# A fused recurrence and gated MLP: the first pairs' sums freed of a shared-tile dependency, all steps in another order, and an earlier gate for the third pair's inputs

## The chip, the cores and the metric

The kernel runs on one core of one Trainium2 chip. The metric is the device time of one execution in microseconds (us), the median of several runs. Five engines work side by side, each with its own queue in program order: TensorE (PE, with the weight loads PEld shown apart), VectorE (DVE), ScalarE (ACT), GpSimd (POOL) and SyncE (SP). Here SP issues nearly all transfers of inputs and outputs, POOL issues the weight transfers, and sixteen DMA engines move the data.

## What is computed

Two parts follow each other. The first is a recurrence with a 48x48 state per batch and head, whose decay differs by row. The second is an MLP on its output, with the gate h cos(h).

```python
batch, n_heads, seq, head_dim = (4, 8, 768, 48)
for t in range(S):
    state = alpha[:, :, t, :, None] * state + np.einsum('bhd,bhe->bhde', k[:, :, t], v[:, :, t])
    y[:, :, t] = np.einsum('bhd,bhde->bhe', q[:, :, t], state)
x = attn_out.transpose(0, 2, 1, 3).reshape(B * S, H * D)   # 3072 x 384
h = x @ w_in            # w_in 384 x 2048
g = h * np.cos(h)
return (g @ w_out)      # w_out 2048 x 384
```

## The kernel before

**Pairs.** The 4 x 768 tokens are cut into 12 *pairs* J of 256 tokens; three pairs make one batch (`NJB = 3`), and the state passes from pair to pair within a batch. Each of the 128 partitions holds two neighbouring tokens, e = 0 and 1. A pair is worked as two chunks c = 0 and 1 of 128 tokens.

**The steps of one pair**, each a small function that issues a handful of instructions:

- `load a|k|q|v` (SP, one DMA of 384 KB each). `ln` (ACT) takes the logarithm of alpha.
- `cums` (PE) sums these logs over the tokens with a triangular matrix. For pairs 0, 1 and 2 the two tokens have their own sums: `cums0` makes those of e = 0 and `cums` those of e = 1, in the two banks of one PSUM tile `cums_h` (`two_banks`). For pairs 3 to 11 `mula` (POOL) multiplies the two tokens' alphas first, `cums` makes one set of sums in the tile `x`, and `sub` (DVE) derives the other.
- `icp J e` and `exps J e` (ACT) read a bank of sums and write exp of minus and plus the sums. For pairs 3 to 11 `eb` is all four of them and then `ln` of the next pair.
- `sk J e`, `sq J e` scale k and q by these (kh, qh), on POOL or DVE. `castv` (POOL) casts v; `vst` (four DMAs from SP) or, for pairs 0 to 2, `vpe` (PE) with `vev` (ACT) stacks it in another order. `decay` (POOL) prepares the factors of the state.
- `trans` (PE, 32 transposes), `evT J c` (DVE or ACT, the copy of a bank to qkT), `scores J c` (PE), `mask J c` (DVE), `outer` (PE, the pair's additions to the state, U), `add` (DVE) and `state` (POOL) carry the state on.
- `yT` (PE) makes the output of the recurrence, transposed; `evy J c` copies it to xT.
- The MLP: `m1 J u` for u = 0 to 3 (PE, 12 matmuls of 256 columns, 512 hidden features), `sin` (ACT, the cosine), `gate` (DVE, the product), then `m2 J c part` (PE, 4 matmuls of 384 columns), `evo J c` (copy) and `out J c` (store).

In the profile a step is seen by its line and its tile: `cums` L160 and L172, `icp` L197, `exps` L205, `trans` L272, `scores` L287, `outer` L305, `yT` L354, `m1` L374, `sin` L380, `gate` L385, `m2` L403. The weights come in eight blocks, `w1 u` (L126) and `w2 u` (L132), called W1.u and W2.u below; m1 of block u needs W1.u, and part u of m2 needs W2.u.

**PSUM.** The tag `h` has three buffers of two banks, shared by `cums_h`, U, the stacked v, the transposes T, the scores A, y and the hidden tile h. A new tile waits until all readers of the buffer's previous tile are done. The tags `x` and `o` have one buffer each; so m2 of the next chunk waits for the copy of the last one.

**Order.** Nothing is scheduled by the framework: the table `PLAN` (L446 to L511) gives every step of every pair a number, the steps are issued in the order of these numbers, and a letter behind a number names the engine (`12160:D` is DVE). Each engine works through its own share of the list strictly in that order. `IDLE` places matmuls on a tile of zeros between the first steps. Dependencies between steps are found from the tiles that they touch, and a PSUM tile counts as a whole there: an instruction of ACT that reads one bank of `cums_h` comes after every matmul to the other bank that stands before it in the list, and a matmul after every such read.

**The gate.** `GATES` makes the load of alpha of pair 2 (`a`, 2) wait for the last matmul of a step; the loads behind it in SP's queue wait with it:

```python
GATES, AFTER = {("a", 2): ("yT", 1)}, {}
...
if (nm, J) in AFTER:
    tc.add_manual_dep(dma.ins, AFTER[nm, J].ins.name, ...)
```

Of the kernel before, what the change touches and what calls it, by code (L numbers as in the profile page):

```python
# [11 lines left out]
AF = mybir.ActivationFunctionType  # L12
# [4 lines left out]
def kernel(  # L17
# [10 lines left out]
    nc = tc.nc  # L28
    B, H, S, D = q.shape
# [69 lines left out]
    GATES, AFTER = {("a", 2): ("yT", 1)}, {}  # L99
# [57 lines left out]
    def sums(J, t, mats):  # L157
        o = t[:, 0:HD].rearrange("p (h d) -> p h d", h=H)
        for i, m in enumerate(mats):
            nc.tensor.matmul(o, m.rearrange("p c i -> p (c i)"), lna_t[J % NL][:, i, :, 0:D], start=(i == 0),  # L160
                             stop=(i == len(mats) - 1))

    def cums(J):
        if (J, 1) not in cums_ps:
            cums_ps[J, 1] = ps.tile([C, 512], FP, tag="x", name="cums", bufs=1)
        t = cums_ps[J, 1]
        lna = lna_t[J % NL]
        ne = 1 if J in both else 2
        sums(J, t, [tri, tri][:ne])
        for p in range(NP):  # L170
            for e in range(ne):
                nc.tensor.matmul(t[:, HD + 2 * p : HD + 2 * p + 2],  # L172
                                 lna[:, e, 2 * p : 2 * p + 2, :].rearrange("s h d -> s (h d)"), inchunk,
                                 start=(e == 0), stop=(e == ne - 1))
# [4 lines left out]
    def cums0(J):  # L179
        t = two_banks("cums_h")  # L180
        for e in range(2):
            cums_ps[J, e] = t[:, e]
        sums(J, cums_ps[J, 0], [tri, strict])
# [10 lines left out]
    def icp(J, e):  # L194
        act_set("exp")
        icp_sb[J, e] = sb.tile([C, HD], FP, tag=f"icp{e}", name="icp", bufs=BUF["cp"])
        nc.scalar.activation(out=icp_sb[J, e], in_=logs(J, e)[:, 0:HD], func=AF.Exp, scale=-1.0)  # L197

    def exps(J, e):
# [5 lines left out]
        nc.scalar.activation(out=cp_sb[J, e], in_=t[:, 0:w], func=AF.Exp)  # L205
# [219 lines left out]
    def idle(n):  # L425
# [21 lines left out]
        "load a": "1320 1974 27415 27985 34270 40270 43270 54870 67336 68770 70970 93397",  # L447
        "load k": "750 2544 28555 37270 46270 52480 58570 69470 72470 85140 91627 113474",
        "load q": "5250 6750 29125 38770 48970 56370 57870 60070 78470 84570 87104 96187",
        "load v": "3750 8250 35770 41770 51910 61570 67906 73970 75470 85710 95267 96757",  # L450
        "w1": "15334 12769 17804 16954",
        "w2": "11919 20284 19434 21134",
        "mula": "- - - 36680 41180 47582 54280 61956 76220 87867 79850 105765",
        "ln": "6160 7660 35857 38802 - - - - - - - -",
        "cums0": "7065 8565 36762 - - - - - - - - -",
        "cums": "7385 8885 37082 40224 45645 52564 65189 75864 86319 101370 105687 126624",
        "sub": "- - - 41095 48653 53084 68143 79971 86910 101948 106207 127144",
        "icp 0": "8400 10365 37282 - - - - - - - - -",
        "icp 1": "9990 9615 38042 - - - - - - - - -",
        "exps 0": "11510 9085 37657 - - - - - - - - -",  # L460
        "exps 1": "10740 11125 38417 - - - - - - - - -",
        "eb": "- - - 43138 49360 59320 71283 83790 88947 103219 109067 127741",
        "sk 0": "8970:D 11125:D 38180 44230 53330 64626 74150 90547 93387 106715 109595 129364:D",
        "sk 1": "10655:D 10185:D 38612:D 45094:D 52380 60226 77170 88817 96837 110545 113395 132041",
        "sq 0": "12160:D 14753:D 40150:D 45680:D 56671:D 65155:D 78900 85074 95107 111495 112445 133161",
        "sq 1": "12974:D 14283:D 39680:D 45680 55230 63676 75100 86024 91497 114515 116415 129403",
        "castv": "10660 16184 42680 48680 62906 71716 73380 94337 92617 104995 130491 144063",
        "vst": "- - - 49610 63836 82270 79970 98527 102027 109974 131421 151922",
        "vpe": "12269 19888 44159 - - - - - - - - -",
        "vev": "15703:A 20408:A 45777:A - - - - - - - - -",  # L470
        "decay": "11579 11749 45180 49450 56180 80800 76050 92447 114345 115465 132991 146818",
        "trans": "14073 17773 40885 47348 58944 70064 80866 92234 109989 116249 127239 136001",
        "evT 0": "14773:A 18473:A 41585 48048 60976 71899 81566:A 93894 111044 116949:A 129834 138061",
        "evT 1": "16453:A 19403:A 43330 48048:A 59896 72979 81586 93289 112124 117657 128759 137201:A",
        "scores 0": "16168 19573 43514 48885 69514 73578 83495 102418 118225 127719 141861 153101",
        "scores 1": "17553 21293 45302 49948 60920 83715 87697 106082 118445 127019 136481 141641",
        "mask 0": "16608 20013 43954 49603 70759 74158 85295 104038 118665 130439 144246 155872",
        "mask 1": "17993 21808 46625 51218 62056 84155 88867 106682 120280 127619 136921 143106",
        "outer": "11844 21513 43734 50168 69734 87367 83935 102638 115919 118665 142081 152771",
        "add 0": "13808 22948 46150 50743 70284 87917 86435 103563 117182 119805 142631 155397",  # L480
        "add 1": "15551 24515 - 53559 72504 - 88392 107822 - 121420 145386 -",
        "state 0": "14460 23600 46802 51395 70936 89767 87087 104215 121237 120457 143283 156049",
        "state 1": "18654 43450 - 61176 78120 - 96057 115635 - 131261 146038 -",
        "yT": "20503 26545 48000 58219 72693 91349 90719 109104 124433 140168 151138 162701",
        "evy 0": "21333:D 27535:D 49128:D 60501:D 73683 92814:D 91919 110094:D 125423 140998 152879:D 163777:D",
        "evy 1": "21333 27658 48990 59421:D 73683:D 92339:D 91549 110569:D 125793 141368 152128 163814",
        "m1 0": "23356 30719 52864 63871 77482 95445 98081 113200 130658 146436 158652 170128",
        "m1 1": "22038 32037 51246 65489 74546 94127 92809 121714 129340 147754 154722 171446",
        "m1 2": "27430 29401 54182 61235 78800 96763 104369 120396 132629 149072 159970 166198",
        "m1 3": "25132 33355 55500 62553 76164 99399 110564 111882 136796 145118 161288 172764",  # L490
        "sin 0": "24874 32237 54382 65389 79000 96963 99659 114718 132212 147954 160232 171646",
        "sin 1": "23556 33555 52906 67007 76064 95645 94327 123232 131204 149332 156240 172964",
        "sin 2": "28948 30919 55700 62866 80318 98281 106765 121914 134147 150590 161488 167716",
        "sin 3": "26650 40836 57018 64071 77682 100917 112613 113621 138314 146636 162806 174282",
        "gate 0": "26130 33386 55531 67003 80446 98112 100808 116042 133493 149103 161381 172795",
        "gate 1": "24990 37307 54055 68618 77213 96794 95476 124381 132353 150481 157389 174113",
        "gate 2": "30097 32068 57141 64015 82191 99430 108297 125521 135296 151739 162637 168865",
        "gate 3": "28010 42190 58281 65863 78831 102423 113762 114902 139463 147785 164252 175431",
        "m2 0 0": "28748 41460 56818 70639 84360 100717 114518 125318 138114 150390 163586 174082",
        "m2 0 1": "34673 42113 57471 71292 85013 101670 115171 125971 138767 152023 164239 176046",  # L500
        "m2 0 2": "35326 42766 59519 71945 85666 103063 116824 128034 139420 153416 164892 176699",
        "m2 0 3": "35979 44554 60172 73893 86619 103716 117477 128687 140893 154069 165545 177352",
        "m2 1 0": "37612 45947 66807 80118 88012 106397 119090 131976 142506 156040 167516 174735",
        "m2 1 1": "38265 46600 67460 81441 88665 107050 119743 133947 143159 156693 168169 175393",
        "m2 1 2": "38918 49200 68113 82094 89318 107703 123032 134600 143812 157346 168822 178005",
        "m2 1 3": "39571 50593 68766 82747 89971 108356 123685 135253 144465 157999 169475 178658",
        "evo 0": "36832:D 45407 61581:D 78353:D 87472 105178:D 118330 129540 141746 154922:D 166398:D 178205:D",
        "evo 1": "40620:D 52358:D 69619 83600:D 99289 111649:D 124538 136831 148962 159862 170328:D 179531:D",
# [49 lines left out]
```

## Time and profile before

| what | value |
|---|---|
| median of 3 runs | 186.13 us (185.88 to 186.54) |
| the profiled execution | 185.82 us, its span 184.0 us |
| PE busy | 175.6 us, of it 66.8 in m1 (L374) and 66.7 in m2 (L403) by the page |
| DVE, ACT, POOL busy | 134.7, 126.4, 77.3 us |
| ACT table loads | 18 of 1.28 us |
| one load of 384 KB, issue to landing | about 6 us (median) |
| W1 and W2 blocks, issue to landing | 7.1 and 10.2 us (median) |
| first m1 matmul | 21.72 us |
| last PE work ends | 180.9 us |

The page divides the span into 40 slices of 4.6 us; a digit is the busy share in tenths. Busy time of PE is modelled, since matmuls overlap, so a stall is better seen in the distance between the starts of steps. A bracket behind a row of the timeline gives the idle time ahead of it on its engine, and who ended it.

### The profile page before, as it was taken

How to read it: one execution, taken by the hardware profiler on the slowest of the kernel's cores; microseconds unless marked ns; L12 is line 12 of the kernel's file. 1: busy time of each engine (PE TensorE's matmuls, PEld its weight loads, DVE VectorE, ACT ScalarE, POOL GpSimd, SP SyncE). 2: the span in 40 equal slices, each digit the busy share in tenths (PEclk: the TensorE clock that was granted, in tenths of full speed). 3: DMA queues.
4: the chain of work that ended last, by engine and by line, in shares of the span. 5: the costliest groups of instructions: out<-in, count | busy, mean ns of one | idle time of the engine just before them, and what ended most of it. 6: DMA issues, size and time to landing. Idle time of an engine off the chain costs nothing.

```text
span 184.0 us, 5751 instructions
## 1 busy us (share of the span) xinstructions
PE 175.6 (95%) x2469; PEld 125.7 (68%) x2469; DVE 134.7 (73%) x184; ACT 126.4 (69%) x161; POOL 77.3 (42%) x110
## 2 busy tenths in 40 slices
PE   7888899998999999999999999999999999999993
PEld 2435678664687776876688668586876686786872
DVE  7078876589999889599659986975976656763561
ACT  2466976889698986889678999728965273372330
POOL 5079610147763743792994168830550320100000
PEclk9999999999999999999999999999999999999999
DMA  5999999999959999997799943500050004302102
GB/s 148 261 260 164 185 201 226 258 248 264 298 135 278 264 221 233 264 264 198 174 277 266 266 124 86 145 0 4 4 181 8 2 9 138 133 0 75 56 0 86
DMA packets 60137, 29.47 MB, mean 160 GB/s; under 512 B 51024, under 2 KB 60112, under 8 KB 60112
## 3 DMA queue, kind: packets, MB, share of 16 engines
q1 hardware_dynamic: 56256, 25.86, 58.1%
q0 software_dynamic: 3712, 3.15, 11.2%
q8 instruction: 19, 0.31, 0.8%
q10 hardware_dynamic: 144, 0.10, 0.2%
q14 instruction: 6, 0.05, 0.1%
HBM read 25.17 MB, written 4.72 MB: 162 GB/s over the span
## 4 chain that ended last, share of the span: by engine, by line
PE 73%; ACT 16%; DVE 3%; DMA 3%; issue 2%; SPq 1%; POOL 0%
PE h_ps L374 30%; PE o_ps L403 26%; PE y_ps L354 5%; DMA a<-in_alpha_dram 3%; ACT c_sb L380 3%; PE T_ps L272 3%; PE A_ps L287 3%; ACT L141 3%; ACT lna L146 3%; ACT cp L205 2%; ACT L380 2%; ACT qkT L278 2%; PE U_ps L305 2%; ACT icp L197 2%; PE o_last L403 1%
## 5 line engine op out<-in xcount | busy, mean ns | idle before, releaser
L385 DVE TENSOR_TENSOR gsb<-h_ps,c_sb 128x1024 bf16<-128x1024 f32 x48 | 58.0, 1220 | 21.8 <-ACT c_sb L380 21.2
L380 ACT ACTIVATE c_sb<-h_ps,halfpi 128x1024 bf16<-128x1024 f32 x48 | 53.0, 1113 | 27.6 <-PE h_ps L374 24.0
L374 PE MATMUL h_ps<-xT,w 128*128 128x256 bf16 x576 | 66.8, 273 | 0.4 <-DVE us L319 0.3
L403 PE MATMUL o_ps<-w,gsb 128*128 128x384 bf16 x368 | 66.7, 327 | 0.0
L374 PEld LDWEIGHTS <-w 128*128 128x128 bf16 x576 | 55.4, 98 | 9.4 <-issue 0.8
L403 PEld LDWEIGHTS <-gsb 128*128 128x128 bf16 x400 | 36.4, 98 | 21.4 <-DVE gsb L385 0.4
L327 POOL TENSOR_TENSOR un<-us,c 128x384 bf16<-128x384 f32 x20 | 16.7, 836 | 38.4 <-DVE us L319 27.5
L293 DVE TENSOR_TENSOR A_sb<-A_ps,msk 128x1024 bf16<-128x1024 f32 x24 | 28.9, 1213 | 2.0 <-PE A_ps L287 2.0
L217 POOL TENSOR_TENSOR kh<-k,icp 128x384 bf16<-128x384 f32 x17 | 16.9, 1000 | 8.5 <-ACT icp L197 8.5
L221 POOL TENSOR_TENSOR qh<-q,cp 128x384 bf16<-128x384 f32 x15 | 15.3, 1026 | 11.0 <-ACT cp L205 11.0
L154 POOL TENSOR_TENSOR a<-a 128x384 f32<-128x384 f32 x9 | 9.0, 1000 | 13.3 <-DMA a<-in_alpha_dram 13.3
L224 POOL CAST vp<-v 128x768 bf16<-128x768 f32 x12 | 10.1, 839 | 9.3 <-DMA v<-in_v_dram 7.9
L146 ACT ACTIVATE lna<-a 128x768 bf16<-128x768 f32 x12 | 10.2, 846 | 4.7 <-DMA a<-in_alpha_dram 4.7
L429 PE MATMUL idle_ps<-zeros 128*128 128x512 bf16 x40 | 11.5, 429 | 1.2 <-DVE halfpi L77 1.2
L141 ACT ACT_TABLE_LOAD x9 | 11.5, 1283 | 0.9 <-PEq L542 0.7
L278 ACT COPY qkT<-T_ps 128x1024 bf16<-128x1024 bf16 x8 | 8.0, 1015 | 5.9 <-PE T_ps L272 5.8
L380 ACT ACT_TABLE_LOAD x9 | 11.5, 1283 | 0.2
L319 DVE TENSOR_TENSOR us<-U_ps,un 128x384 f32<-128x384 f32 x16 | 8.7, 548 | 3.9 <-PE U_ps L305 2.9
L415 DVE COPY o_sb<-o_ps 128x384 f32<-128x384 f32 x12 | 6.6, 552 | 6.7 <-PE o_ps L403 6.7
L278 DVE COPY qkT<-T_ps 128x1024 bf16<-128x1024 bf16 x16 | 10.7, 675 | 0.0
L287 PE MATMUL A_ps<-qkT 48*128 48x128 bf16 x192 | 9.2, 218 | 1.0 <-ACT vs L244 0.6
L287 PEld LDWEIGHTS <-qkT 48*128 48x128 bf16 x192 | 5.8, 94 | 5.5 <-issue 3.1
(68 smaller groups left out, 153.7 us busy)
## 6 DMA issues: line engine op xcount, KB each, us to landing
k<-in_k_dram SPq DMA_DIRECT2D x12, 384.0 KB, 6.0
a<-in_alpha_dram SPq DMA_DIRECT2D x12, 384.0 KB, 5.7
v<-in_v_dram SPq DMA_DIRECT2D x12, 384.0 KB, 6.2
q<-in_q_dram SPq DMA_DIRECT2D x12, 384.0 KB, 6.3
out_dram<-o_sb SPq DMA_DIRECT2D x23, 192.0 KB, 3.7
vs<-vp SPq DMA_DIRECT2D x36, 64.0 KB, 2.4
w<-in_moe_w_out_dram POOLq DMA_DIRECT2D x4, 384.0 KB, 10.2
w<-in_moe_w_in_dram POOLq DMA_DIRECT2D x4, 384.0 KB, 7.1
```

What stands on the lines that cost most here:

```text
L141: nc.scalar.preload_act_table_set("natural_log_exp_and_others")
L146: nc.scalar.activation(out=lna_t[J % NL][:, :, :, 0:D].rearrange("p e h d -> p h e d"), in_=a_sb.pop(J), func=AF.Ln)
L217: eng.tensor_tensor(out=kh_t[J % NQ][:, e, :, 0:D], in0=kqv["k", J][:, :, e], in1=icp_, op=ALU.mult)
L221: eng.tensor_tensor(out=qh_t[J % NQ][:, e, :, 0:D], in0=kqv["q", J][:, :, e], in1=cp, op=ALU.mult)
L278: ins = copy(out=qkT_sb[J][:, c], in_=T_ps[J][:, c].rearrange("r n e s -> r n (e s)"))
L287: last = nc.tensor.matmul(A_ps[J, c][:, a, p, :], qkT[r, c, NP + p, :], qkT[r, c, p, :], start=True, stop=True)
L293: nc.vector.tensor_tensor(out=A_sb[J][:, c].rearrange("s a p t -> s (a p) t"), in0=A_ps.pop((J, c)).rearrange("s a p t -> s (a p) t"), in1 ...
L327: nc.gpsimd.tensor_tensor(out=u, in0=U_sum.pop(n), in1=c2_sb[J][:, :, c].unsqueeze(3).to_broadcast([C, NP, 2, D]), op=ALU.mult)
L374: nc.tensor.matmul(h_ps[J, u][:, f, :], w1[:, kk, ft * C : (ft + 1) * C], xT[J][:, kk, :], start=(kk == 0), stop=(kk == KT - 1))
L380: nc.scalar.activation(out=c_sb[J, u], in_=h_ps[J, u], func=AF.Sin, bias=halfpi, scale=1.0)
L385: nc.vector.tensor_tensor(out=gsb[J][:, u * FW : (u + 1) * FW], in0=h_ps.pop((J, u)), in1=c_sb.pop((J, u)), op=ALU.mult)
L403: nc.tensor.matmul(o[:, 0 : cols.stop - cols.start], gsb[J][:, ft, c * C : (c + 1) * C], w2[:, ft, cols], start=(done == 1 and ft == fts[0 ...
```

## The change

Three things are changed. First, for pairs 0 to 2 the matmuls and the reads of the two banks of `cums_h` are recorded by token (`use`), and an ACT read of one token's bank and a PE write of the other's are declared free of each other. Second, the gate of pair 2's alpha is the step `yT` of pair 0 in place of pair 1. Third, `PLAN` and `IDLE` are new throughout: every step has another number, and some have another engine.

```diff
-    GATES, AFTER = {("a", 2): ("yT", 1)}, {}
+    GATES, AFTER = {("a", 2): ("yT", 0)}, {}
...
+    users = {}
+
+    def use(J, e, ins, pe=False):
+        for e2, pe2, other in users.setdefault(J, []):
+            if e2 != e and pe2 != pe:
+                tc.declare_no_dep(ins.ins, other.ins, reason="the two tokens' sums lie in banks of their own")
+        users[J].append((e, pe, ins))
+
-    def sums(J, t, mats):
+    def sums(J, t, mats, e=1):
...
+            if (J, 0) in cums_ps:
+                use(J, e, ins, pe=True)
...
-        sums(J, cums_ps[J, 0], [tri, strict])
+        sums(J, cums_ps[J, 0], [tri, strict], e=0)
...
-        nc.scalar.activation(out=icp_sb[J, e], in_=logs(J, e)[:, 0:HD], func=AF.Exp, scale=-1.0)
+        ins = nc.scalar.activation(out=icp_sb[J, e], in_=logs(J, e)[:, 0:HD], func=AF.Exp, scale=-1.0)
+        if (J, 0) in cums_ps:
+            use(J, e, ins)
```

The matmuls of `cums` and the ACT instruction of `exps` are recorded in the same way. Of the plan, the rows that the steps below speak of (one number per pair, 0 to 11; the old row above the new one):

```diff
-        "load a": "1320 1974 27415 27985 34270 40270 43270 54870 67336 68770 70970 93397",
+        "load a": "10 30 960 1010 1230 1770 2160 1940 2610 3070 3560 3090",
-        "load k": "750 2544 28555 37270 46270 52480 58570 69470 72470 85140 91627 113474",
+        "load k": "40 150 1140 1490 1990 2230 2050 3290 2740 4070 3580 4640",
-        "w1": "15334 12769 17804 16954",
+        "w1": "400 380 500 160 - - - - - - - -",
-        "w2": "11919 20284 19434 21134",
+        "w2": "650 1000 490 970 - - - - - - - -",
-        "sk 1": "10655:D 10185:D 38612:D 45094:D 52380 60226 77170 88817 96837 110545 113395 132041",
+        "sk 1": "250:D 320:D 1220 1580 2100 2320 2890 3300 3660 4300 4470 5300",
-        "sq 0": "12160:D 14753:D 40150:D 45680:D 56671:D 65155:D 78900 85074 95107 111495 112445 133161",
+        "sq 0": "330:D 470 1130:D 1610 2110 2520 2860 3460 3640 4290 4340 5150",
-        "trans": "14073 17773 40885 47348 58944 70064 80866 92234 109989 116249 127239 136001",
+        "trans": "350 510 1330 1630 2120 2550 3040 3480 4370 4630 5060 5320",
-        "outer": "11844 21513 43734 50168 69734 87367 83935 102638 115919 118665 142081 152771",
+        "outer": "260 630 1320 1720 2660 3260 3220 4110 4620 4710 5450 5700",
-        "yT": "20503 26545 48000 58219 72693 91349 90719 109104 124433 140168 151138 162701",
+        "yT": "590 720 1660 2130 2800 3650 3600 4250 4900 5400 5630 5840",
-        "m1 0": "23356 30719 52864 63871 77482 95445 98081 113200 130658 146436 158652 170128",
+        "m1 0": "770 860 1900 2440 2990 3840 3850 4540 5210 5790 6070 6360",
...
-    IDLE = [(1501, 16), (7915, 1), (9416, 8), (12569, 4), (14554, 5), (16389, 3), (18254, 3)]
+    IDLE = [(45, 10), (175, 5), (255, 7), (345, 4), (405, 3), (505, 3), (535, 5), (555, 2)]
```

In the new list the queues read so. SP: a0 a1 k0 v0 q0 k1 q1 v1, then (behind the gate) a2 a3 v2 q2 k2 a4 k3 q3 v3; before: k0 a0 a1 k1 v0 q0 q1 v1, then a2 a3 k2 q2 a4 v2 k3 q3 a5 v3. POOL issues the weight blocks as W1.3, W1.1, W1.0, W2.2, W1.2, W2.0, W2.3, W2.1; before: W2.0, W1.1, W1.0, W1.3, W1.2, W2.2, W2.1, W2.3. PE's first MLP steps are m1 0 1, yT1, m1 0 0, m1 0 3, m1 0 2, m1 1 0, m1 1 2, m1 1 1, m2 0 0 0, m2 0 0 2, m2 0 0 3, m1 1 3, m2 0 0 1, then cums0 2.

## The prediction

> **What bounds the kernel now.** I read the page's totals and its 40 slices first, then the chain of waits, then busy time by stretches.
>
> ```profile
> span 184.0 us, 5751 instructions
> ...
> PE 175.6 (95%) x2469; PEld 125.7 (68%) x2469; DVE 134.7 (73%) x184; ACT 126.4 (69%) x161; POOL 77.3 (42%) x110
> ...
> PE   7888899998999999999999999999999999999993
> ...
> DMA  5999999999959999997799943500050004302102
> ...
> PE 73%; ACT 16%; DVE 3%; DMA 3%; issue 2%; SPq 1%; POOL 0%
> ```
>
> TensorE (PE) sets the time: short of 9 tenths only in the first five slices (23 us) and once near 45 us. DMA is full as well, but only until about 105 us. The stretches say where the two matter (columns: busy us and instructions of PE, PEld, DVE, ACT, POOL, then granted clock, DMA share, GB/s):
>
> ```profile
> 2.50:14.20 11.70, 10.29 (x103) 4.84 (x101) 6.25 (x23) 4.87 (x10) 4.19 (x10) 1.00 1.24 264
> 14.20:15.20 1.00, 1.00 (x17) 0.44 (x8) 1.00 (x2) 0.81 (x1) 1.00 (x2) 1.00 0.82 49
> 15.20:30.80 15.60, 13.99 (x260) 10.44 (x259) 12.03 (x14) 11.50 (x14) 6.83 (x9) 1.00 1.25 196
> 30.80:44.00 13.20, 12.84 (x139) 8.96 (x136) 9.11 (x13) 11.64 (x14) 4.61 (x5) 1.00 1.12 257
> ...
> 40.00:60.00 20.00, 19.27 (x352) 13.55 (x352) 19.18 (x25) 17.88 (x23) 12.63 (x16) 1.00 1.01 246
> 60.00:80.00 20.00, 19.98 (x286) 15.22 (x279) 16.59 (x23) 16.61 (x23) 12.14 (x15) 1.00 1.12 247
> ...
> 140.00:160.00 20.00, 20.00 (x271) 14.16 (x269) 13.30 (x15) 8.65 (x11) 3.44 (x5) 1.00 0.21 65
> ```
>
> Eight input loads fill 2.5 to 14.2, there is a hole of one us, then the eight weight blocks alone run to 30.8 and the next pairs' inputs follow. From 60 us on PE is full. DVE is nearly full from 40 to 60. The clock is 1.00 throughout. The timeline around the change:
>
> ```profile
> 9.44 0.49 ACT L205 ACTIVATE cp<-cums_h 128x384 f32<-128x384 f32 x1 [0.70 <-PE cums_h L172]
> ...
> 21.72 2.78 PE L374 MATMUL h_ps<-xT,w 128*128 128x256 bf16 x24
> ...
> 27.21 0.99 SPq L110 DMA_DIRECT2D a<-in_alpha_dram  x2
> 28.25 4.49 SPq L110 DMA_DIRECT2D k<-in_k_dram  x1
> ...
> 43.64 0.51 PE L305 MATMUL U_ps<-vp,kh 64*128 64x96 bf16 x8 [0.23 <-POOL un L327]
> 46.13 0.32 PE L160 MATMUL cums<-lna,tri 128*128 128x384 bf16 x1 [0.36 <-ACT lna L146]
> ```
>
> I also measured every matmul step's start-to-start time against its quickest form (m1 1.31, m2 0.65, y 0.90, trans 0.57, outer 0.34, scores 0.33 us). The excess over the run is 10.9 us: 5.3 before the first m1 (21.72), 0.46 after "m10 0", 1.4 in five places from 43.0 to 46.2, 0.59 at 116.9, and crumbs of 0.1 or so. A new order can gain only an earlier 21.72 and those.
>
> **The change part by part.**
>
> *The cut dependency.* It removes ACT's wait for the other bank's sums: the 0.70 above and 1.1 at an icp (one wait each), about 0.5 a session, the length of "cums". In the first pair the next thing late is the loads (below), so alone it is worth 0 to 0.5 at the start and nothing at the end; I take 0.
>
> *Filler matmuls.* 40 become 39, all before the first m1, under waits for loads: 0.
>
> *Work moved between engines.* By the instruction lists six qh products leave DVE for POOL (9 to 3), one kh goes from POOL to DVE, one qkT copy and four xT copies go from ACT to DVE, and ACT loads tables 16 times in place of 18. With the means of the rows: DVE -6x0.73+0.67+0.68+4x0.58 = -0.7; ACT -1.02-4x0.59-2x1.28 = -5.9; POOL +6x1.03-1.00 = +5.2 us. None of the three bounds the run; what they give is slack, so 0 by itself. Where the cover is gone (DVE from 40 to 60) it is in the walk below.
>
> *First loads and weights.* SP now issues a0 a1 k0 v0 q0 k1 q1 v1 (before k0 a0 a1 k1 v0 q0 q1 v1). The trace's landings, 4.47 5.99 7.49 9.01 10.51 12.02 13.51 14.86, go to the new order: a0 at 4.47 (was 5.99), k1 at 12.02 (was 9.01). POOL issues W1.3 right after the first decay, near 9, not W2.0 at 12.5; so the hole at 14.2 closes: 0.8 of DMA time.
>
> *To the first m1.* DVE has sk1 1 ahead of sq0 0, so k1 matters: 12.02+0.56+0.55 = 13.15, trans0 to 13.8. ACT: evT0 0 to 14.9, exps1 0 to 15.35; POOL sq1 0 to 16.4; trans1 to 17.05 (was 18.1). ACT's two evT1 copies end at 19.1, yT0 runs 19.3 to 20.1, its copies end at 20.75, m1 starts near 21.0: -0.7.
>
> *To the third pair.* PE then has yT1 (waits for mask1 1, 22.5), eight m1 and the m2 steps; 35.2 at "m20 0 1" against 36.4 now, if weights land as now or sooner. But the next steps need inputs of pair 2. From 14.2 on DMA owes eight weight blocks (17.9 us for eight in the trace, 15.25 to 33.2) and a2 a3 v2 q2 k2 at 1.5 each: the fifth lands at 39.4, in whatever order. Now the fifth (a4) lands at 40.43. k2 is last of the five: sk2 1 on POOL ends at 40.5, outer2 and trans2 at 41.4. Now trans2 ends at 40.97 with outer2 (0.34) still to do: equal work at 41.3. So the 0.7 and the rest of the lead are lost waiting for k2: +0.1.
>
> *The gate.* a2 and a3 wait for yT0 (about 20.1), not yT1 (27.16), and SP's queue behind them (v2 q2 k2) moves with them. In the trace that wait costs nothing: a2 is issued at 27.21, yet its first packet moves at 30.83, when the weights run out; the SP queue behind stalls 4.49. So I price the earlier gate at 0 if queued weights go first. After it, though, POOL still has W2.0, W2.3 and W2.1 to issue (20 to 24), behind three loads already queued. Served in order of issue, W2.3 lands at 34.6 (wanted 32.6), W2.1 at 36.8 (wanted 34.6), outer2 at 41.2, not 40.5: bounds 0 to +0.7; I take 0, by the row at 30.83.
>
> By the Trainium skill, "DMA: Bandwidth & Descriptors", Queues, rings and completion order, each DMA engine goes round between queues packet by packet. The row at 30.83 speaks against it here: no input packet for 2.5 us while weights were queued. By that rule the weights share from 20 on; what that gives is the first rival.
>
> *Pairs 2 and 3.* After trans2 PE has four m2, vpe2, two scores2, two m2 and cums4 (5.1 us) to trans3: 46.5; POOL's chain (k3 42.4, sk3 1, sq3 1, sq3 0) ends at 45.9, so it fits. trans3 starts at 47.89 now, with the five stalls ahead of it: a lead of 1.4, so 1.5 gained since trans2. Then DVE limits: mask2 1 to 47.8 holds yT2, state3 0 and mask3 0 (53.8) hold m12 2; yT3 starts at 58.5 with trans4 behind it, against 58.92 with trans4 to come; the fourth m1 of pair 3 ends at 67.4 with one m2 more than now at 67.63. The lead there is 0.9, so 0.5 is given back.
>
> *The rest, 67 to 181.* The matmuls are the same. The stall of 0.59 at outer8 may go; on the other side yT8 comes 1.55 us of PE work after its last scores (5.56 now) while a mask takes 1.21, yT5 2.03 (7.06). Bounds -0.6 to +1.5; I take 0. The end (last m2 pieces, half copies, store) is the same.
>
> Sum: three times 0 for the cut, the fillers and the moved work, 0.1 - 1.5 + 0.5 for the three stretches, 0 for the gate and the rest: -0.9. The profiled execution took 185.82 (span 184.0 and 1.8 around it), 0.31 under the median 186.13. 184.9 on its own scale, **185.2** as a median.
>
> **Rivals.**
>
> *The weights come late (slower).* If the third pair's loads, freed 7 us earlier, take the engines ahead of or beside W2.0, W2.3, W2.1, "m20 0 1" waits for W2.1 and all of PE behind it. With all five loads ahead it lands at 39.4, outer2 starts 0.65+3.7 later, 43.75: 3.2 more than forecast; half of that if they share. It decides from a landing of W2.1 at 37. For it: W2.3 and W2.1 are issued behind the loads. Against: the row at 30.83. 186.8 to 188.4, say 187.5. A W1.3 that slows k1, q1, v1 adds to it (v1 at 19 would put the first m1 at 22.0 or later, hidden until the wait for k2).
>
> *DVE becomes the bound (no change).* From 42 to 62 its rows sum to 24.0 us in the new order, over 20 us of PE work (now 21.0). My walk lets 0.5 through; if all but 2.5 us of slack comes through, it is 1.5: 186.1.
>
> *The cut dependency does nothing and the gate does more.* If k2 lands sooner than 39.4 (weights pushed back just to where they are wanted), the lead of 1.2 at 35 us is kept and comes on top of the forecast: 184.0.
>
> **How the numbers follow.** Forecast 0.40 (184.4 to 185.5), larger gain 0.15, no change 0.17, slower 0.28 (weights 0.20, late masks and inputs 0.08). A measurement here tells 0.3%, 0.56 us, from nothing: faster 0.55, same 0.17, slower 0.28. The range 183.5 to 187.7 leaves out about 0.1 on each side.
>
> **What would show it.** First m1 near 21.0; a0 first at 4.5; first packet of a2 when weights run out, or else at 21 to 22; W2.1's landing against 34.6; outer2 waiting for kh near 40.5; trans3 near 46.5; no stalls of 0.3 from 41 to 47. A first a2 packet at 21 with PE waiting in the m2 steps near 33 to 38 would make it wrong, and so would PE waits for A_sb masks after 67.

## The result and the profile after

| | before | after |
|---|---|---|
| median (lowest to highest), 20 runs each | 186.41 us (185.82 to 187.57) | 188.62 us (185.90 to 193.86) |
| profiled execution, its span | 185.82, 184.0 us | 189.06, 187.3 us |
| mean granted clock in it | 1.00 | 0.982 |

The ratio after to before is 1.0066, 95% interval 1.0045 to 1.0088: slower. The plain medians lie further apart (1.012), since the ratio leaves out runs more than 1.5% above the fastest of their kernel, which nine of the changed kernel's 20 are, the profiled one among them. Its runs also spread far more than those of before, and they go with their clock in the main: the one of 20 with a mean granted clock of 1.0 took 185.9 us, those at 0.991 mostly 187.0 to 188.6, those at 0.982 188.7 to 189.7. That clock is the first hint.

The page of the changed kernel, its totals, slices and shares of the chain:

```profile
span 187.3 us, 5751 instructions
...
PE 177.2 (95%) x2468; PEld 126.8 (68%) x2468; DVE 136.8 (73%) x185; ACT 121.3 (65%) x153; POOL 82.7 (44%) x115
...
PE   7959999999999999999999999999994999999993
...
PEclk9996999999999999999999999999998799999999
...
PE 85%; DMA 4%; SPq 4%; DVE 3%; issue 1%; DVEq 0%
```

ACT has left the chain (16% before), as the cut dependency and the moved copies should have it. But two things are new, and both stand in the same place: PE's row has a 4 in its 31st slice (140.5 to 145.2 us), where before PE was full from 60 us to the end, and the clock is down in the 31st and 32nd (and in the 4th, near 15 us). In the chain 4% each fall to DMA and to SP's queue (3% and 1% before), but by the page's lines only 1% of each belongs to this place, to `vs` and L246; the rest are loads of the first pairs.

The timeline around it, SP and PE (start, duration, engine, line, operation, count; in brackets the idle time ahead of it and who ended it):

```profile
119.96 19.08 SPq L246 DMA_DIRECT2D vs<-vp  x8
...
130.44 1.60 POOL L240 CAST vp<-v 128x768 bf16<-128x768 f32 x2
...
134.82 0.63 PE L370 MATMUL y_ps<-A_sb,vs 128*32 128x128 bf16 x32
...
...
139.72 2.39 SPq L246 DMA_DIRECT2D vs<-vp  x4
140.18 0.52 PE L370 MATMUL y_ps<-qkT,un 128*32 128x128 bf16 x24
143.00 0.29 PE L370 MATMUL y_ps<-A_sb,vs 128*32 128x128 bf16 x5 [2.30 <-DMA vs<-vp]
143.62 0.57 PE L370 MATMUL y_ps<-A_sb,vs 128*32 128x128 bf16 x27 [0.33 <-DMA vs<-vp]
```

yT10 (L370) begins at 140.18 and needs pair 10's stacked v, `vs`. That is four transfers from SP (L246, the step vst10), and they are issued only at 139.72, though their source was cast on POOL by 132.04 (the row at 130.44 is the casts of pairs 10 and 11). What held SP is the first row: eight transfers, those of pair 9 and then those of **pair 11**, with SP waiting inside that row (asked from 126 us on, the timeline has pair 11's four by themselves, from 135.48 to 139.04). Pair 11 writes the same buffer as pair 9 (`NS` = 2 buffers, and 9 and 11 are both odd), so its transfers wait for the matmuls of yT9 that read it (the row at 134.82). In the new plan vst11 has number 5470 and vst10 5620: SP takes them in that order, then the store, and vst10 last. yT10 takes 3.94 us from its first matmul to the next step in place of 0.90: 3.04 lost.

Then the clock. Busy time by stretches (columns as in the prediction's):

```profile
12.00:14.20 2.20, 0.50 (x17) 0.29 (x16) 2.19 (x3) 0.04 (x1) 2.18 (x4) 1.00 1.25 222
14.20:16.00 1.80, 1.79 (x21) 0.60 (x23) 1.58 (x3) 1.31 (x2) 0.83 (x1) 0.57 1.19 278
...
140.00:143.00 3.00, 0.70 (x27) 0.38 (x25) 1.18 (x3) 0.00 (x0) 0.83 (x1) 1.00 0.55 149
...
144.50:146.50 2.00, 2.00 (x18) 1.23 (x13) 1.96 (x3) 0.34 (x1) 0.00 (x0) 0.50 0.21 76
146.50:148.00 1.50, 1.50 (x10) 1.12 (x9) 0.00 (x0) 0.00 (x0) 0.83 (x1) 0.64 0.00 0
```

PE runs 0.70 us of the three from 140 to 143; soon after, at 144.16, the granted clock falls to 0.50 and stays there for 3.41 us. The steps in it (scores and outer of pair 11 together, an m2 step of pair 8, an m1 step of pair 9) take 0.51, 0.60 and 0.51 us longer than their quickest form: another 1.6. The same is seen after 12.0 to 14.2, where trans0 waits for DVE. So 3.04 + 1.6 = 4.7 us lost, less the lead of 0.9 that the kernel did have up to there, is +3.8; the last matmul step starts 3.2 us later than before (183.31 against 180.11), the other 0.6 being won back behind.

### The profile page after: what moved, and what is told of

Same layout as the page of the kernel before. It is cut to its first block, busy times and chain, and to the rows that moved or that the text cites. A ratio compares the mean times of both kernels' runs of the same rounds, so it can differ in the third digit from the quotient of the medians.

```text
span 187.3 us, 5751 instructions
## 1 busy us (share of the span) xinstructions
PE 177.2 (95%) x2468; PEld 126.8 (68%) x2468; DVE 136.8 (73%) x185; ACT 121.3 (65%) x153; POOL 82.7 (44%) x115
## 3 DMA queue, kind: packets, MB, share of 16 engines
q0 software_dynamic: 3712, 3.15, 10.6%
## 4 chain that ended last, share of the span: by engine, by line
PE 85%; DMA 4%; SPq 4%; DVE 3%; issue 1%; DVEq 0%
PE h_ps L390 34%; PE o_ps L419 31%; PE y_ps L370 5%; PE A_ps L303 4%; DMA k<-in_k_dram 3%; PE T_ps L288 3%; PE U_ps L321 3%; SPq L110 3%; PE idle_ps L445 2%; PE o_last L419 1%; DVE A_sb L309 1%; DVE kh L233 1%; DMA vs<-vp 1%; SPq L246 1%; PE cums L168 1%
## 5 line engine op out<-in xcount | busy, mean ns | idle before, releaser
L390 PE MATMUL h_ps<-xT,w 128*128 128x256 bf16 x576 | 67.8, 274 | 0.1
L419 PE MATMUL o_ps<-w,gsb 128*128 128x384 bf16 x368 | 67.7, 329 | 0.0
L390 PEld LDWEIGHTS <-w 128*128 128x128 bf16 x576 | 56.0, 98 | 9.6 <-issue 0.4
L237 POOL TENSOR_TENSOR qh<-q,cp 128x384 bf16<-128x384 f32 x21 | 21.4, 1032 | 6.3 <-ACT cp L219 6.3
L431 DVE COPY o_sb<-o_ps 128x384 f32<-128x384 f32 x13 | 7.2, 552 | 9.6 <-PE o_ps L419 9.6
L294 ACT COPY qkT<-T_ps 128x1024 bf16<-128x1024 bf16 x7 | 7.0, 1012 | 10.4 <-PE T_ps L288 10.4
L445 PE MATMUL idle_ps<-zeros 128*128 128x512 bf16 x39 | 12.3, 458 | 1.2 <-DVE halfpi L77 1.2
L379 DVE CAST xT<-y_ps 128x384 bf16<-128x384 f32 x16 | 8.9, 580 | 4.7 <-PE y_ps L370 4.6
L370 PE MATMUL y_ps<-A_sb,vs 128*32 128x128 bf16 x384 | 7.9, 219 | 3.1 <-DMA vs<-vp 2.6
L141 ACT ACT_TABLE_LOAD x8 | 10.3, 1283 | 0.9 <-PEq L558 0.7
L396 ACT ACT_TABLE_LOAD x8 | 10.3, 1283 | 0.1
L379 ACT CAST xT<-y_ps 128x384 bf16<-128x384 f32 x8 | 4.7, 592 | 7.4 <-PE y_ps L370 7.4
```

The costliest lines, as they stand in the source:

```text
L237: eng.tensor_tensor(out=qh_t[J % NQ][:, e, :, 0:D], in0=kqv["q", J][:, :, e], in1=cp, op=ALU.mult)
L294: ins = copy(out=qkT_sb[J][:, c], in_=T_ps[J][:, c].rearrange("r n e s -> r n (e s)"))
L370: last = nc.tensor.matmul(y_ps[J][32 * g : 32 * g + 32, c, i * C : (i + 1) * C], l, r, start=(c, g) not in begun, stop=(c, g, i) not in ou ...
L379: ins = copy(out=xT[J][:, :, c * C : (c + 1) * C].rearrange("r i (t e) -> r i e t", e=2), in_=y_ps[J][:, c, 0 : KT * C].rearrange("r (i e ...
L390: nc.tensor.matmul(h_ps[J, u][:, f, :], w1[:, kk, ft * C : (ft + 1) * C], xT[J][:, kk, :], start=(kk == 0), stop=(kk == KT - 1))
L396: nc.scalar.activation(out=c_sb[J, u], in_=h_ps[J, u], func=AF.Sin, bias=halfpi, scale=1.0)
```

## The experiments

"Pair 11's transfers first" is undone, the clock is held up without undoing it, and each of the other parts of the change is made or unmade alone. All kernels were timed in five rounds against the kernel before.

**Pair 10's transfers ahead of pair 11's.** One row of the plan:

```diff
-        "vst": "- - - 2090 2310 3450 3230 4120 4700 5390 5620 5470",
+        "vst": "- - - 2090 2310 3450 3230 4120 4700 5390 5465 5620",
```

> The changed kernel with vst of pair 10 issued ahead of vst of pair 11 (5465 and 5620 in the plan). Theory A (SP's queue): in the changed kernel yT10 stands still for 3.0 us because vst10 is queued behind vst11, which waits for yT9 (135.4) and then takes 3.6 us to issue; castv10 was done at 132. With the order turned, vst10 issues at about 132 to 134 and lands before 139, yT10 takes 0.9 and not 3.94 us, the clock stays at 1.00 near 144, and the kernel is 3.0 + 1.7 = 4 to 5 us faster than the changed one: about 184, faster than the kernel before by 1 to 2 us. Theory B (the change lost its time at the start, by late m1 and the gate): no more than 0.5 us moves.

Measured: 184.69 us median (184.59 to 184.84, 6 runs), ratio to before 0.9921 (0.9903 to 0.9939); profiled span 182.8, clock 1.000. The timeline of this kernel, SP and PE:

```profile
131.50 2.38 SPq L246 DMA_DIRECT2D vs<-vp  x4
...
135.70 2.97 SPq L246 DMA_DIRECT2D vs<-vp  x4
...
140.40 0.52 PE L370 MATMUL y_ps<-qkT,un 128*32 128x128 bf16 x24
140.75 0.62 PE L370 MATMUL y_ps<-A_sb,vs 128*32 128x128 bf16 x32
```

Pair 10's transfers go out at 131.50, pair 11's at 135.70 when yT9 is done, and yT10 has no bracket: its 56 matmuls start within 0.9 us. The span is 4.5 us shorter, against the 4.7 read off the trace above, and the clock drop near 144 is gone with the wait. Over all runs the swap is worth less than in these two profiles: 3.9 us by the medians, and 2.7 by the ratios (1.0066 to 0.9921). The order of two rows in one queue turns the change from a loss into a gain of 0.8%.

**The wait kept, PE busy through it.** Thirteen matmuls on zeros ahead of yT10, into a tile of their own use:

```diff
+    def late_idle(n):
+        t = ps.tile([C, 512], FP, tag="x", name="late_ps", bufs=1)
+        for _ in range(n):
+            nc.tensor.matmul(t, zeros[:, 0:C], zeros, start=True, stop=True)
...
+    order.append((5625, len(order), "late", [13]))
```

> The changed kernel with 13 matmuls on zeros ahead of yT10 (2.8 us at the full clock), so that PE works where it stood still; vst10 is as late as ever. Theory A: yT10 still waits until 143 to 143.6, but the granted clock stays at 1.00 from 144 to 148, where it was 0.50 for 3.4 us: 1.7 us faster than the changed kernel in runs that had that drop. Theory C (the low clock near 144 has another cause than PE's standstill): the drop stays, no gain.

Measured: 188.05 us (187.03 to 191.51, 6 runs), ratio 1.0093 (1.0062 to 1.0123); profiled span 185.9, against 187.3 without them. Timeline and stretches of this kernel:

```profile
139.96 2.38 SPq L246 DMA_DIRECT2D vs<-vp  x4
...
140.39 2.97 PE L444 MATMUL late_ps<-zeros 128*128 128x512 bf16 x13
...
143.29 0.52 PE L370 MATMUL y_ps<-qkT,un 128*32 128x128 bf16 x24
```

```profile
140.00:143.00 3.00, 3.00 (x17) 1.37 (x14) 1.48 (x3) 0.00 (x0) 0.83 (x1) 1.00 0.56 150
...
144.50:146.50 2.00, 2.00 (x28) 1.58 (x25) 2.00 (x3) 0.57 (x1) 0.00 (x0) 1.00 0.35 117
146.50:148.00 1.50, 1.50 (x15) 1.15 (x13) 0.14 (x1) 0.81 (x1) 0.83 (x1) 1.00 0.00 0
```

The transfers are as late as before and yT10 waits behind the zeros until 143.29, so the 3 us stay; but the clock is 1.00 from 144.5 to 148, where it was 0.50 and 0.64, and PE starts 28 and 15 matmuls there in place of 18 and 10. From the scores behind yT10 to the second m2 step after them PE takes 2.64 us (144.35 to 146.99) in place of 4.25 (144.12 to 148.37), and the span is 1.4 shorter. So in these two profiles the drop goes with PE's standstill. In time the gain isn't shown: the medians are 188.05 and 188.62, with overlapping spreads, and the ratios 1.0093 and 1.0066. Three of the six runs have a mean clock of 1.0, of the changed kernel's 20 only one; but these three took 187.0 to 188.7 us and that one 185.9. That the zeros cost time of their own where the wait is shorter would explain it, and isn't shown.

**The gate back at yT1, the rest as changed.**

```diff
-    GATES, AFTER = {("a", 2): ("yT", 0)}, {}
+    GATES, AFTER = {("a", 2): ("yT", 1)}, {}
```

> The changed kernel with the third pair's loads gated by yT1 again (about 25 and not 21.9). If the earlier gate costs (weights late): W2.3 and W2.1 land about 3 us sooner than 31.95 and 34.91 and PE gains at the m2 steps near 33 to 36. If transfers go in the order of their issue and all of them have to be done by the time of k2: W2.1 sooner, k2 still at 38 to 39, the first 45 us the same within 0.5 us, and the time as the changed kernel's within 1 us.

Measured: 189.67 us (188.17 to 190.56, 6 runs), ratio 1.0186 (1.0149 to 1.0222). It doesn't tell what the gate is worth: in its profile outer2, the first step to need pair 2's k, starts at 40.00 and so earlier than in the changed kernel (40.63), while yT10 loses 3.34 us and the clock falls at 143.4 for 6.83 us, twice as long. The late mishap covers what was to be measured, and the test was made again without it:

**The gate back at yT1, with vst10 first** (both edits shown above).

> vst_swap (the changed kernel with vst10 ahead of vst11) with the gate at yT1 again, so that the wait at yT10 no longer hides what the gate does. If transfers go in the order of their issue: W2.3 and W2.1 go ahead of a2 and a3, k2 still lands with the last of the same 13 transfers, outer2 starts at 40.0 to 40.5 and the time is within 0.3% of vst_swap's 184.7. If the earlier gate is what gives the new order its lead: 1 us or more slower than vst_swap.

Measured: 184.87 us (183.57 to 186.23, 8 runs), ratio 0.9914 (0.9885 to 0.9944), against 0.9921 with the early gate. The earlier gate is worth nothing that can be measured here.

**The early gate alone, in the kernel before.**

```diff
-    GATES, AFTER = {("a", 2): ("yT", 1)}, {}
+    GATES, AFTER = {("a", 2): ("yT", 0)}, {}
```

> The kernel before with the gate at yT0 and nothing else. If transfers go in the order of their issue: all weights are issued by 21.2 there, about when the gate opens, so hardly any load passes a weight block and the time is within 0.3% of the kernel before. If loads and weights share, or loads go first: m2 steps near 34 wait and it is 0.5 to 2 us slower.

Measured: 186.67 us (185.89 to 187.58, 12 runs), ratio 1.0012 (0.9996 to 1.0028): no difference in the old order either. But the first theory's reason doesn't hold. The DMA queues of this kernel from 26 to 33 us (packets, MB, share of the 16 engines; q0 has the weights, 3.15 MB in the whole run, q1 the transfers that SP issues):

```profile
q0 software_dynamic: 1252, 0.94, 85.3%
q1 hardware_dynamic: 1252, 0.47, 38.9%
```

Both queues move the same number of packets, so loads and weights take turns here, whichever was issued first. A weight packet is twice as large (about 750 bytes, a load's 384), so the weights keep two thirds of the traffic. Their last block lands at 35.69 in place of 33.19, and that costs PE at most 0.1 us: the twelve m2 matmuls at 34.3 take 2.21 us and not 2.11.

**The cut dependency alone, in the kernel before** (old plan, old gate; the code of `use` and its calls added).

> The kernel before, its plan and its gate, with the cut dependency alone. Theory: what it lets start sooner waits for the loads next, so within 0.3% of the kernel before (186.1 to 186.7), at most 0.5 us sooner at the first m1. Rival: the order of the first pairs' ACT work changes in its favour, and 0.5 to 1 us come through to the end.

Measured: 185.78 us (185.22 to 187.11, 12 runs), ratio 0.9975 (0.9953 to 0.9997); profiled span 183.4 against 184.0. In its trace trans0 starts at 13.44 (13.72 before) and the first m1 at 21.44 (21.72), trans3 at 47.11 (47.89), and 0.64 of it is left at the end. A small gain, about 0.5 us.

**The new plan without the cut**, with vst10 first, so that the wait at 140 doesn't cover it:

```diff
-            if e2 != e and pe2 != pe:
+            if False:
...
-        "vst": "- - - 2090 2310 3450 3230 4120 4700 5390 5620 5470",
+        "vst": "- - - 2090 2310 3450 3230 4120 4700 5390 5465 5620",
```

> vst_swap without the cut dependency, the order of every queue the same. cut_old showed 0.28 us at the start and 0.5 us near 42 to 47 for the cut on the old plan. In the new plan two ACT steps (exps0 0, icp0 0) stand ahead of the matmuls of cums0, which then have to wait for them. Theory: 0.3 to 1 us slower than vst_swap (185.0 to 185.7). Rival: the third pair waits for k2 in any case and the start is under that wait: the same.

Measured: 187.09 us (185.18 to 187.97, 12 runs), ratio 1.0018 (0.9988 to 1.0048), against 0.9921 with the cut; profiled span 184.1 against 182.8. The timeline of this kernel:

```profile
6.83 0.48 PE L168 MATMUL cums_h<-lna,tri 128*128 128x384 bf16 x2 [0.96 <-ACT icp L209]
...
38.58 0.48 PE L168 MATMUL cums_h<-lna,tri 128*128 128x384 bf16 x2 [2.10 <-ACT cp L219]
```

Here PE, not ACT, is the one that waits: the sums of token 1 (L168) wait until ACT has read the sums of token 0 out of the other bank, 0.96 us at the start and 2.10 at pair 2, where the same matmuls start at 36.34 with the cut. In the new plan exps2 0 (1110) stands ahead of cums2 (1150), so the false dependency lies on the path of the engine that bounds the run. There the cut is worth 1.3 us by the spans and 2.4 by the medians, and by the ratio nothing is left of the new plan's gain without it. The median mixes two groups: five of the twelve runs have a mean clock of 0.998 or more and took 185.2 to 186.1 us, seven have 0.991 and took 187.0 to 188.0. So the waits themselves cost about 1.2 us (185.84, the median of the five, against 184.69), and the rest goes with a fall of the clock that the profile, taken at 1.0, doesn't show.

**vst10 first, and sq0 0 ahead of sk1 1 on DVE**, to take away the wait of trans0 seen at 12.0 to 14.2:

```diff
-        "sq 0": "330:D 470 1130:D 1610 2110 2520 2860 3460 3640 4290 4340 5150",
+        "sq 0": "315:D 470 1130:D 1610 2110 2520 2860 3460 3640 4290 4340 5150",
```

> vst_swap with sq0 0 ahead of sk1 1 on DVE, so that q of the first pair is scaled at 11 to 12 and not behind k1 (12.0 to 14.15 in the changed kernel). Theory: trans0 runs in one piece near 12.1 to 12.7, PE's gap of 1.9 us inside it and with it every drop of the clock near 14 go; the first m1 is 0.5 to 1 us sooner, but outer2 waits for k2 as before, so the end moves by less than 0.3 us (184.4 to 184.8). Rival: 0.5 us or more comes through to the end.

Measured: 184.86 us (183.96 to 185.77, 6 runs), ratio 0.9915 (0.9887 to 0.9943): the same as with vst10 first alone. The first m1 starts at 20.85 in place of 21.83, and all six runs have a clock of 1.0, where four of the six with vst10 first alone had 0.988 to 0.991; neither comes through. trans2 ends at 41.80 against 42.00, since PE has to wait for inputs of the next pairs anyway. The timeline of this kernel:

```profile
36.16 0.84 ACT L146 ACTIVATE lna<-a 128x768 bf16<-128x768 f32 x1 [1.58 <-POOL a L154]
...
37.42 1.46 PE L419 MATMUL o_ps<-w,gsb 128*128 128x384 bf16 x8 [1.20 <-ACT o_sb L431]
...
40.87 0.38 PE L321 MATMUL U_ps<-vp,kh 64*128 64x96 bf16 x5 [0.28 <-POOL kh L233]
```

Most of the lead goes at 37.42: alpha of pair 3 lands at 35.06, POOL multiplies it, ACT waits 1.58 for that with `ln`, and the copy of o that m2 needs stands behind `ln` in ACT's queue. The wait for k of pair 2 (`kh`, L321 is outer2) takes another 0.28. With vst10 first alone the two waits are 0.55 and 0.34.

## Why the prediction was wrong

**What failed** is the step *the rest, 67 to 181*: "The matmuls are the same … Bounds -0.6 to +1.5; I take 0". I compared PE's order and the masks from DVE and ACT there, and not SP's queue, though the plan's rows were at hand. In the profiled execution the step had to be +3.0 for vst10 behind vst11, and +1.6 for the clock after it. `vst_swap` undoes the two together: 184.69, with the prediction at 185.2 (by the ratio -1.5 us against before, where the sum had -0.9). No rival had that mechanism; the slower one (weights late, 187.5) had the direction but another place.

**The cut dependency**, "I take 0", was mis-sized. Alone it is worth 0.64 us at the end of the profiled execution (ratio 0.9975), since the first wait it takes away moves trans0 by 0.28 and later ones the rest. And I priced it by the waits that the old order had, not by those that the new order would have without it: 0.96 and 2.10 at PE, and 1.2 us at the full clock (2.4 by the medians).

**Work moved between engines.** Busy time changed by -5.1 us on ACT (-5.9 forecast), +5.4 on POOL (+5.2) and +2.1 on DVE (-0.7).

**First loads and weights.** a0 landed at 4.39, k1 at 11.92 (4.47 and 12.02 forecast) and the hole at 14.2 closed: DMA share 1.25 and 1.19 in the stretches at 12.0 and 14.2. Right.

**To the first m1.** 22.64 against 21.0 forecast; wrong by 1.6. The timeline of the changed kernel shows why:

```profile
12.81 1.34 DVE L237 TENSOR_TENSOR qh<-q,cp 128x384 bf16<-128x384 f32 x1
...
14.21 0.44 PE L288 MATMUL T_ps<-ident_bf,qh 64*128 64x64 bf16 x16 [1.71 <-DVE qh L237]
```

DVE's product qh took 1.34 us where I had put 0.55, trans0 waited 1.71 for it, and the clock was 0.50 from 14.45 to 17.87. Why that product is slow is open. POOL issues two weight blocks at the same time (12.42, 1.58 us), but that alone isn't the cause: in the kernel before two such products took 1.03 together (from 12.40) while POOL issued W2.0 (12.50, 0.93). It cost nothing in the end, as `both` shows.

**To the third pair.** The times were right: k2 landed at 38.61 (39.4 forecast), outer2 started at 40.63 (40.5). That a lead is lost to waits for inputs was right too, but the wait for k2 is the smaller part of it: in `both` it takes 0.28 and the wait behind pair 3's alpha 1.20, and in the changed kernel, whose m1 was 1.6 late, outer2 has no wait at all. That 40.63 lies so close to the forecast was luck in part.

**The gate**, taken as 0 with bounds of 0 to +0.7, was right in its price (`swap_gate_y1` and `gate_y0_old`) and wrong in its reason, so this was luck. I took the row at 30.83 to say that queued weights go first. But in all ten traces a2's first packet moves 3.1 to 4.1 us after its issue (27.21 to 30.82 before, 21.90 to 25.24 in the changed kernel), while the first load of a run, with nothing else under way, needs 1.1; and in the kernel before the last weight packet moves at 32.70, so the weights had not run out at 30.83. What makes the delay is open. Once both queues move they take turns, as the two rows of `gate_y0_old` show. By the Trainium skill, "DMA: Bandwidth & Descriptors", Queues, rings and completion order, each DMA engine goes round between queues packet by packet; the trace agrees, with 1252 packets of each. So the first rival had the mechanism right, and its price wrong: W2.3 landed at 31.95 and W2.1 at 34.91 (34.6 and 36.8 at worst by my sum), before PE came to them, where the rival needed W2.1 after 37.

**Pairs 2 and 3.** trans3 at 46.8 (46.5), yT3 at 59.0 (58.5), and the excess of PE's steps before yT10 comes to 9.44 us against 10.3 to 10.4: the lead of 0.9 that I had forecast stood until 140 us. DVE didn't become the bound.

## What to carry to other kernels

When a plan is renumbered, read every queue that can wait, those of the engines that only issue transfers too: for each transfer ask which buffer it writes, who reads that buffer last, and what stands behind it. A transfer that waits for a buffer holds back ready ones behind it, and on the bounding engine a standstill of some 2 us can be paid for a second time by the clock. A dependency that is cut is to be priced in the new order, by the waits which that order would have with it. And two times that agree in one trace, like the end of the weights and the first packet of a2, aren't yet a cause: look whether they still agree in a second kernel.

## What was not expected of the hardware

**The clock falls after a short standstill, and it matters where that lies.** In the changed kernel's trace the granted clock changes at 14.45, 17.87, 144.16 and 147.57 us, that is 3.41, 37 times 3.41 and 3.41 apart. In the other nine its changes are whole multiples of 3.41 us apart, too. The work in such periods of 3.41 us, in the changed kernel and then in the one with vst10 first (columns as above):

```profile
11.04:14.45 3.41, 1.70 (x40) 0.84 (x36) 2.90 (x4) 0.80 (x1) 3.23 (x5) 1.00 1.25 231
14.45:17.87 3.41, 3.41 (x34) 1.39 (x26) 2.13 (x4) 1.41 (x2) 2.27 (x3) 0.50 1.22 245
...
140.75:144.16 3.41, 0.83 (x34) 0.58 (x36) 0.43 (x1) 0.00 (x0) 0.83 (x1) 1.00 0.62 173
144.16:147.57 3.41, 3.41 (x28) 2.33 (x26) 2.21 (x3) 0.58 (x1) 0.83 (x1) 0.50 0.23 82
```

```profile
10.18:13.59 3.41, 2.49 (x42) 1.17 (x40) 1.96 (x3) 0.94 (x2) 3.24 (x6) 1.00 1.27 245
13.59:17.00 3.41, 2.39 (x38) 1.16 (x38) 3.02 (x5) 1.41 (x2) 2.28 (x3) 1.00 1.21 245
```

trans0 waits 1.71 us in both kernels. In the first the wait lies in one period, PE is busy for 1.70 us of it, and the clock is 0.50 in the next. In the second a boundary cuts the wait in two, and the clock stays.

Over all ten traces, from the first clock change on and while PE has work left, PE was busy for 0.83, 1.12, 1.66, 1.70 and 1.70 us in the periods ahead of a drop, and for 1.99 or more in the others, except for one of 1.62 without a drop (`swap_nocut`, from 34.76). So, as far as ten traces and a modelled busy time can say, a standstill of about half a period is enough if it lies within one, and where the boundaries lie differs from run to run. What ends a drop is open: in the kernel with the gate back, whose waits at yT10 were 2.23 and 0.33 us, the clock stayed low for 6.83 us, though PE was busy for 3.15 of the first 3.41. The Trainium skill, "TensorE: Matmul & The Clock Gate", Part 1, has a free-running window of about 3.4 us and warns of idle gaps longer than that. The window agrees with the traces; the warning is too mild for these runs, where 2.6 us in all at yT10, and 1.7 near 14 us, were enough.

**The wait itself varies.** The one execution of the changed kernel with a clock of 1.0 took 185.9 us, 1.2 above the kernel with vst10 first, so it can't have lost the 3.04 us of the profiled one in full; it has no trace.
